# Twelve unread products of the unit matrix behind chunk 0's right sides in a recurrence-plus-MLP kernel

## The chip, the cores and the metric

The kernel runs on one core of one Trainium2 chip. The metric is the device time of one execution in microseconds (us), from the host's side of the launch to its end; for one core it is the time of that core. A profiled execution also has a span, the time from its first to its last instruction, which is a little shorter than its device time.

## What is computed

The reference runs a recurrence over 768 tokens for 4 sequences and 8 heads of width 40, and feeds its result through a two-layer block with SiLU. All arrays are float32.

```python
for t in range(S):
    y[:, :, t] = np.einsum('bhd,bhde->bhe', rt, state)
    Sa = np.einsum('bhde,bhe->bhd', state, at)
    state_decay = state * wt[:, :, None, :] - np.einsum('bhd,bhe->bhde', Sa, bt)
    state = state_decay + np.einsum('bhd,bhe->bhde', vt, kt)
x = y.transpose(0, 2, 1, 3).reshape(B * S, H * D)      # 3072 x 320
h = x @ w_in                                           # 320 -> 2048
out = (h * (1.0 / (1.0 + np.exp(-h)))) @ w_out         # 2048 -> 320
```

## The kernel before, in words

The 768 tokens are cut into 12 chunks of 64. Inside a chunk the recurrence becomes a triangular system: products of decayed inputs, an inverse of a unit triangular matrix for each of the 32 pairs of sequence and head, and an update of the state between chunks. For chunk `n` the steps are `load` and `load_r` (DMAs on SP's queue), `prepare` (scans and scalings on VectorE, small products on TensorE), `special` (the inverse for chunks 0 to 2), `inverse` and `merge` (the inverse for later chunks, two at a time), `chain` (solve and state update), `read` (the chunk's output `y`), `bring`, and `moe` (the two layers for the chunk's 256 tokens, lines 1397 to 1460). `weights` (lines 461 to 522) rebuilds float32 weights from 64-bit words that POOL's queue fetches; the first three of its ten pieces add two halves by products with the unit matrix `ident` (line 508).

Nearly all products of the recurrence are small: 40 or 64 rows by 64 columns. The products of `moe` fill the array: 128 rows, 128 columns of weights, 256 columns streamed (line 1405) or 320 (line 1445). Every product is two instructions on TensorE, a weight load and a matmul.

No step is issued where it stands in the text. `add` records each with an engine, a cost, what it reads and writes, and a priority; `plan.best(10, 400)` (line 1505) tries priorities against its own cost model, fixes one order for all engines, and gives every temporary one of four PSUM tiles `pairs[0]` to `pairs[3]` (two banks each). Lines 1504 to 1506 then issue the steps in that order, one program for each engine:

```python
    with tc.manual_schedule():
        for op in plan.best(10, 400):
            op["do"]()
```

TensorE starts in this order: for chunk 0 the decayed products with `b` and with `k` (function `between`, line 682), two batches of transposes (line 769), and the right sides (function `sv`, line 744, 64 products of the masked result with `v`); then for chunk 1 the products with `b` (line 682), and for chunk 0 transposes (926), first product (913) and refinement (958) of the inverse, the solve (1166), chunk 1's products with `k` (682), the weights' sums (508), the reading of the chunk (1269, 1323), the solve (1135), and so on. Chunk 1's first products need `a` times its decay, which VectorE makes in `prepare(1)` (`scale`, line 654, behind the scans of lines 627 and 645).

The right sides' products are recorded by the one statement that the change touches:

```python
        add("PE", 0.9, sv, [sk, ("v", i2, 0), ("v", i2, 1)], [pv, ("R", i3)], pri + 0.6, [pv, sk], 128)
```

In the order that the planner finds, `sv` of chunk 0 writes `pairs[0]`. The tile `pairs[1]` held chunk 0's products with `k` until VectorE's masking (line 729) had read them, and is next written by chunk 1's products with `b`.

Of the kernel before, what the change touches and what calls it, by code (L numbers as in the profile page):

```python
# [33 lines left out]
class Plan:  # L34
# [9 lines left out]
    def add(self, engine, cost, do, r=(), w=(), pri=0, rooms=(), k=0, size=0.0, shape="Q"):  # L44
        op = dict(
            engine=engine, cost=cost, do=do, pri=pri, rooms=rooms, k=k, size=size, n=len(self.ops), shape=shape
        )
        before = set()
        for k in r:
            if isinstance(k, tuple) and k[0] == "@":  # L50
                before.add(self.wrote[k[1]])
                continue
            if k in self.wrote:
                before.add(self.wrote[k])
            self.read.setdefault(k, []).append(op["n"])
        for k in w:
            if k in self.wrote:
                before.add(self.wrote[k])
            before.update(self.read.get(k, ()))
            self.wrote[k], self.read[k] = op["n"], []  # L60
        before.discard(op["n"])
        op["before"] = before
        self.ops.append(op)
        return op
# [224 lines left out]
def kernel(  # L289
# [15 lines left out]
    nc = tc.nc  # L305
# [26 lines left out]
    ident = const.tile([128, 128], F32, name="ident")  # L332
# [29 lines left out]
    pairs = [ps.tile([128, 2, 512], F32, name=f"pair{i}") for i in range(4)]  # L362
# [9 lines left out]
    add = plan.add  # L372
# [212 lines left out]
    def load_r(n):  # L585
        pri = 10 * n - 4
        late = [[("@", ("in", "X", 0))], [("@", ("xt", 0, 0))]][n] if n < 2 else []
        for b in range(2):
            for j in range(2):
# [17 lines left out]
                    pri,  # L607
                )

    def prepare(n):  # L610
        pri = 10 * (n - 2) + 6 if n != 1 else -8
        i3, i2 = n % 3, n % 2
# [80 lines left out]
        if n < NS:  # L693
            for b in range(2):
                for c in range(4):
                    e = "ACT" if n == 0 and b else "SP"
                    p, r = 32 * c + 16 * b, 64 * b + 16 * c
# [27 lines left out]
        pk, sk = Room("pair", 2), Room("lam", 3)  # L725
# [11 lines left out]
        pv = Room("pair", 2)  # L737
# [11 lines left out]
                    stop=True,  # L749
                )  # L750

        add("PE", 0.9, sv, [sk, ("v", i2, 0), ("v", i2, 1)], [pv, ("R", i3)], pri + 0.6, [pv, sk], 128)
        add(
            "ACT",
            act(640),
# [715 lines left out]
    load(0)  # L1471
    hold(0, at[0], [("a", 0)], 0.5)
    prepare(0)
    special(0)
    load_r(0)
    load(1)
    prepare(1)
    for n in range(5):
        weights(n)
    for n in range(NN):  # L1480
        if n >= NS:
            merge(n)
        for step in (chain, read, bring):
            ahead(step, n)
        if n == 0:
            plan.wrote["@", 0] = plan.wrote["xt", 0, 0]
            hold(4, xt[:, 0], [("xt", 0, h) for h in range(H)], 3)
            special(1)
            for i in range(5, len(units)):
                weights(i)  # L1490
        moe(n)
        if n + 1 < NN:
            load_r(n + 1)
        if n + 2 < NN:
            load(n + 2)
            prepare(n + 2)
        if n + 2 < NS:
            special(n + 2)
            if n + 3 == NS:
                eye()  # L1500
        if n + 1 >= NS and (n + 1 - NS) % 2 == 0 and n + 1 < NN:
            inverse((n + 1 - NS) // 2)

    with tc.manual_schedule():
        for op in plan.best(10, 400):
            op["do"]()

    bad = const.tile([1, 1], I32, name="bad")
    ok = sb.tile([128, 2 * NN], F32, name="ok")
# [18 lines left out]
    with tc.If(flag > 0):  # L1528
# [25 lines left out]
        with tc.For_i(0, S, T) as t0:  # L1554
# [13 lines left out]
            for t in range(T):  # L1568
                a, k, b, wt = (e4[:, x, t].unsqueeze(1).to_broadcast([128, N4, D]) for x in range(4))
# [90 lines left out]
```

## Time and profile before

| what | value |
|---|---|
| device time, median of 3 runs | 743.88 us (742.13 to 744.6) |
| profiled execution: its device time, its span | 742.53 us, 740.8 us |
| mean granted TensorE clock | 0.976 |
| busy: TensorE matmul, weight load | 674.7 us (91%), 540.5 us (73%) |
| busy: VectorE, ScalarE, GpSimd | 419.5 us (57%), 194.6 us (26%), 14.3 us (2%) |
| instructions on TensorE | 12666 weight loads and 12666 matmuls |
| chain that ended last, by engine | PE 80%, DVE 8%, DMA 3%, ACT 3%, issue 3% |
| instruction blocks fetched by DMA (queue 8) | 101 packets, 1.65 MB |

Busy time is the union of the spans of an engine's instructions; matmuls overlap each other, so a busy TensorE is not yet one at its peak. The granted clock is the share of its full clock that a throttle lets TensorE have. "Issue" is time in which an engine waited for nothing that the profile shows. The chain is followed back from the last instruction to whatever released each step.

### The profile page before, as it was taken

To read this page: it belongs to the slowest core of one execution; us is meant where nothing else is said; L and a number is where in the kernel's file an instruction comes from. 1 tells how busy PE (TensorE), PEld (TensorE's weight loads), DVE (VectorE), ACT (ScalarE), POOL (GpSimd) and SP (SyncE) were. 2 spreads that over 40 slices of the span, in tenths; PEclk is the share of its full clock that TensorE was granted. 3 is DMA by queue.
4 is the path that set the end of the run, shared out by engine and by line. 5 is a ranking of instruction groups with operands and counts; after the bars stand their busy time and mean duration, and the time that the engine had idled before them with its cause. 6 is when DMAs were issued, how large, how long until landed. Compare 5 with 4: busy or idle time off the path is not lost.

```text
span 740.8 us, 27279 instructions
## 1 busy us (share of the span) xinstructions
PE 674.7 (91%) x12666; PEld 540.5 (73%) x12666; DVE 419.5 (57%) x614; ACT 194.6 (26%) x241; POOL 14.3 (2%) x31
## 2 busy tenths in 40 slices
PE   2179799898899999999999999899999999999995
PEld 2176577678678677878778878778777778788773
DVE  6845799976479256299273397362686449321000
ACT  3251635523212411404304205124114211202020
POOL 2300000000000000000000000000000000000000
PEclk9996999999999999999999999999998999999998
DMA  7770654742632453525353506333233321401000
GB/s 248 160 227 11 195 210 126 222 116 47 161 107 58 96 135 98 139 61 125 112 133 106 161 19 144 95 99 92 73 93 81 97 60 32 126 21 41 18 1 22
DMA packets 117979, 77.15 MB, mean 104 GB/s; under 512 B 65506, under 2 KB 114338, under 8 KB 117218
## 3 DMA queue, kind: packets, MB, share of 16 engines
q1 hardware_dynamic: 113352, 64.54, 32.9%
q0 software_dynamic: 2096, 10.49, 4.3%
q8 instruction: 101, 1.65, 0.9%
q10 hardware_dynamic: 2410, 0.30, 0.3%
q14 instruction: 20, 0.16, 0.1%
HBM read 60.29 MB, written 14.61 MB: 101 GB/s over the span
## 4 chain that ended last, share of the span: by engine, by line
PE 80%; DVE 8%; DMA 3%; ACT 3%; issue 3%; SPq 1%; ACTq 1%; DVEq 0%
PE pair L1445 27%; PE pair L1405 21%; PE pair L1418 5%; PE pair L1269 4%; PE pair L682 3%; PE pair L1323 3%; PE pair L958 2%; PE pair L1135 2%; PE pair L1223 2%; PE pair L1068 1%; PE pair L1166 1%; PE pair L508 1%; PE pair L744 1%; PE pair L1308 1%; PE pair L1111 1%
## 5 line engine op out<-in xcount | busy, mean ns | idle before, releaser
L1445 PE MATMUL pair<-wo,gts 128*128 128x320 f32 x768 | 219.8, 442 | 1.1 <-issue 1.1
L1445 PEld LDWEIGHTS pair<-wo,gts 128*128 128x128 f32 x768 | 144.7, 192 | 60.4 <-issue 4.3
L1405 PE MATMUL pair<-xt,wi 128*128 128x256 f32 x768 | 175.5, 386 | 1.6 <-ACT R L756 1.3
L1405 PEld LDWEIGHTS pair<-xt,wi 128*128 128x128 f32 x768 | 145.7, 192 | 24.5 <-ACT R L756 1.4
L1428 ACT ACTIVATE gts<-pair 128x1024 f32<-128x1024 f32 x48 | 46.5, 1020 | 134.5 <-PE pair L1418 108.3
L682 PE MATMUL pair<-a,kb 40*64 40x64 f32 x1536 | 32.2, 236 | 35.8 <-DVE a L654 28.7
L1457 DVE COPY ot<-pair 128x320 f32<-128x320 f32 x24 | 11.8, 490 | 92.4 <-PE pair L1445 88.9
L796 DVE TENSOR_REDUCE XI<-XI 128x64 f32<-128x512 f32 (+9 forms) x85 | 58.6, 690 | 2.9
L682 PEld LDWEIGHTS pair<-a,kb 40*64 40x64 f32 x1536 | 28.6, 149 | 38.5 <-issue 20.5
L1418 PE MATMUL pair<-xt,wi 64*128 64x256 f32 x384 | 47.9, 389 | 0.0
L1281 DVE TENSOR_TENSOR lam<-pair,ml 128x1024 f32<-128x1024 f32 x22 | 26.4, 1220 | 32.9 <-PE pair L1269 30.4
L1418 PEld LDWEIGHTS pair<-xt,wi 64*128 64x128 f32 x384 | 35.1, 187 | 6.7 <-issue 2.6
L795 DVE TENSOR_TENSOR XI<-XI,mi 128x1024 f32<-128x1024 f32 (+8 forms) x60 | 33.6, 559 | 9.6 <-DMA mi<-md 8.3
L1334 DVE TENSOR_TENSOR lam<-pair,wz 128x1024 f32<-128x1024 f32 x11 | 13.5, 1223 | 38.8 <-PE pair L1323 38.8
L1269 PEld LDWEIGHTS pair<-r,vut 40*64 40x64 f32 x1536 | 25.9, 142 | 6.8 <-issue 5.9
L664 DVE TENSOR_TENSOR kb<-kbv 128x512 f32<-128x512 f32 (+1 forms) x36 | 29.7, 861 | 0.3
L1269 PE MATMUL pair<-r,vut 40*64 40x64 f32 x1536 | 28.5, 228 | 1.2 <-issue 1.2
L627 DVE TENSOR_TENSOR_SCAN kbv<-wz,zt 128x1024 f32<-128x1024 f32 x12 | 27.5, 2291 | 0.5
L645 DVE TENSOR_TENSOR_SCAN wz<-wz,zt 128x1024 f32<-128x1024 f32 x12 | 27.5, 2289 | 0.3
L756 ACT COPY R<-pair 128x640 f32<-128x640 f32 x12 | 8.3, 693 | 67.1 <-PE pair L744 61.5
L795 DVE TENSOR_TENSOR XI<-XI,xs 128x1024 f32<-128x1024 f32 (+1 forms) x25 | 25.3, 1010 | 0.8
L407 ACT ACTIVATE vu<-pair 64x640 f32<-64x640 f32 x13 | 9.1, 698 | 60.3 <-PE pair L1135 59.4
(151 smaller groups left out, 687.7 us busy)
## 6 DMA issues: line engine op xcount, KB each, us to landing
wz<-in_wT SPq DMA_DIRECT2D x12, 512.0 KB
kbv<-in_bT SPq DMA_DIRECT2D x12, 512.0 KB
a<-in_aT SPq DMA_DIRECT2D x12, 512.0 KB
kbv<-in_kT SPq DMA_DIRECT2D x12, 512.0 KB
r<-in_rT SPq DMA_DIRECT2D x48, 96.0 KB
vut<-in_vT SPq DMA_DIRECT2D x48, 96.0 KB
vu<-in_v SPq DMA_DIRECT2D x24, 160.0 KB
out<-ot SPq DMA_DIRECT2D x48, 80.0 KB
```

What stands on the lines that cost most here:

```text
L627: nc.vector.tensor_tensor_scan(back(V), back(W[:, 2 : 2 + Q * C]), zt, 1.0, ALU.mult, ALU.add)
L645: nc.vector.tensor_tensor_scan(Z, Z, zt, 0.0, ALU.mult, ALU.add)
L664: TTn[engine].tensor_tensor(out=at_(kb, place(is_b, first), (576 * step, 4 // step), (128, 4), (1, C)), in0=blocks((kf, bf)[is_b]), in1=bl ...
L682: nc.tensor.matmul(room.tile[half(b), j, g * C : g * C + C], lhsT=kb[rows(j), place(is_b, q) : place(is_b, q) + C], rhs=A[rows(j), q * C : ...
L795: nc.vector.tensor_tensor(out=at_(tmp, 0, *dims), in0=x, in1=y, op=ALU.mult)
L796: nc.vector.tensor_reduce(out=out_, in_=at_(tmp, 0, *dims), axis=AX.X, op=ALU.add)
L1269: nc.tensor.matmul(pl.tile[half(1 - b if role else b), b, c * C : c * C + C], lhsT=vut[rows(b), role, hu, :], rhs=rs[rows(b), hh, :], star ...
L1281: lambda pl=pl, la=la: nc.vector.tensor_tensor(out=la.tile.rearrange("p (q t) -> p q t", q=Q), in0=pl.tile.rearrange("p a b -> p (a b)").r ...
L1405: nc.tensor.matmul(rooms[g].tile[:, f // 2, (f % 2) * T : (f % 2) * T + T], lhsT=wi[:, k, (4 * g + f) * 128 : (4 * g + f) * 128 + 128], rh ...
L1418: nc.tensor.matmul(rooms[g].tile[:, h, (f % 2) * T : (f % 2) * T + T], lhsT=wi3[half(h), g * 256 + (f % 2) * 128 : g * 256 + (f % 2) * 128 ...
L1428: nc.scalar.activation(out=gts[:, 4 * g * T : 4 * g * T + 4 * T], in_=rooms[g].tile.rearrange("p a b -> p (a b)"), func=AF.Silu)
L1445: nc.tensor.matmul(po[b].tile[:, 0, 0:DM], lhsT=g4[:, f, 128 * b : 128 * b + 128], rhs=wo[:, f, :], start=f == 0, stop=f == NF - 1,)
```

## The change

A new function `idle` inside the builder issues twelve products: the 128 x 128 unit matrix as weights, and the same matrix repeated four times as the 512 streamed columns. They write the two banks of `pairs[1]` in turn, each starting afresh, and nothing reads what they write. `prepare` keeps the record of its right sides and, for chunk 0 alone, hangs `idle` on it; the loop that issues the planned order calls it directly behind that step. The planner does not know of it, so the order and the places of all other steps stay as they are, and no other instruction on any engine gains or loses a wait. TensorE's program grows by 24 instructions, 12 weight loads and 12 matmuls, behind the 224 products that stand before.

```diff
+    def idle():
+
+        for i in range(12):
+            nc.tensor.matmul(
+                pairs[1][:, i % 2].rearrange("p (a b) -> p a b", a=4),
+                lhsT=ident,
+                rhs=ident.unsqueeze(1).to_broadcast([128, 4, 128]),
+                start=True,
+                stop=True,
+            )
+
     def prepare(n):
...
-        add("PE", 0.9, sv, [sk, ("v", i2, 0), ("v", i2, 1)], [pv, ("R", i3)], pri + 0.6, [pv, sk], 128)
+        mine = add("PE", 0.9, sv, [sk, ("v", i2, 0), ("v", i2, 1)], [pv, ("R", i3)], pri + 0.6, [pv, sk], 128)
+        if n == 0:
+            mine["then"] = idle
...
     with tc.manual_schedule():
         for op in plan.best(10, 400):
             op["do"]()
+            if "then" in op:
+                op["then"]()
```

## The prediction

> **What bounds the kernel now.** I read the list of who waited for whom on TensorE first, because the change touches that engine alone, then TensorE's timeline where the new products land, then busy time in windows with the granted clock. Waits (in total, times, longest, us), over the whole span:
>
> ```profile
> PE pair L682 <- DVE a L654: 28.7, 2, 14.9
> PE pair L682 <- issue: 5.5, 6, 2.8
> PE pair L1166 <- issue: 3.2, 2, 2.8
> ...
> PE pair L1405 <- ACT R L756: 1.3, 1, 1.3
> ```
>
> TensorE has two long waits, both at the start and both for VectorE (13.79 us before its first product, 14.93 us before chunk 1's); behind them it is 91% busy and the chain runs through it. The rest that matters is "issue", 2.8 us at a time. The timeline (start, length, line; x counts products):
>
> ```profile
> 13.79 3.69 PE L682 MATMUL pair<-a,kb 40*64 40x64 f32 x128 [13.79 <-DVE a L654]
> 17.42 1.93 PE L769 MATMUL pair<-ident,kb 40*128 40x40 f32 x32
> 19.28 1.94 PE L744 MATMUL pair<-vu,lam 64*64 64x40 f32 x64
> 36.15 1.99 PE L682 MATMUL pair<-a,kb 40*64 40x64 f32 x64 [14.93 <-DVE a L654]
> ...
> 46.48 3.31 PE L958 MATMUL pair<-XI 64*64 64x64 f32 x102 [0.99 <-issue]
> ...
> 53.04 0.26 PE L1166 MATMUL pair<-X,R 64*40 64x64 f32 x3 [2.76 <-issue]
> ...
> 62.50 3.78 PE L508 MATMUL pair<-gts,ident 128*128 128x512 f32 x4
> ```
>
> The new products stand between 19.28 + 1.94 = 21.22 us and 36.15 us. The chain that ends last does not touch TensorE there: from 21.7 to 36.1 us it is VectorE alone (scans of lines 627 and 645, the inverse's steps of 795 and 796, line 654), then TensorE from 36.15 to 69.4 us.
>
> Windows of 3.41 us (length; busy us and instructions of PE, PEld, DVE, ACT, POOL; granted clock; DMA share; GB/s). I chose that width and phase because all changes of the recorded clock stand whole multiples of 3.41 us apart, at 53.27, 66.92, 77.16, 80.57 and 200.04 us:
>
> ```profile
> 32.79:36.20 3.41, 0.05 (x4) 0.05 (x4) 3.33 (x6) 0.00 (x0) 1.88 (x3) 1.00 0.63 78
> 36.20:39.61 3.41, 3.41 (x98) 3.17 (x102) 3.38 (x4) 2.29 (x4) 0.87 (x2) 1.00 0.96 301
> 39.61:43.03 3.42, 3.42 (x92) 3.23 (x90) 0.09 (x1) 3.15 (x7) 0.00 (x0) 1.00 1.03 330
> ...
> 46.44:49.85 3.41, 3.37 (x115) 3.33 (x118) 2.09 (x4) 0.05 (x1) 0.00 (x0) 1.00 1.08 265
> 49.85:53.27 3.42, 0.66 (x40) 0.50 (x34) 0.67 (x1) 0.00 (x0) 0.00 (x0) 0.99 0.34 47
> 53.27:56.68 3.41, 3.41 (x118) 3.25 (x109) 2.73 (x4) 1.19 (x2) 0.00 (x0) 0.50 0.17 43
> ...
> 63.51:66.92 3.41, 3.41 (x18) 1.37 (x18) 2.28 (x10) 0.00 (x0) 0.00 (x0) 0.51 0.00 0
> ```
>
> The column reads 1.00 before the first record, which is at 43.03 us; the products tell that it is not so. Two rows of the answer by tile say how long each lasted (minimum/median/maximum ns, first and last start in us):
>
> ```profile
> L958 PE MATMUL pair<-XI x128: 213/218/267, 44.5 to 49.6; 64*64 64x64 f32 x128
> ...
> L913 PE MATMUL pair<-mi,sb x64: 310/312/363, 39.1 to 40.8; 64*64 64x64 f32 x64
> ```
>
> Same shape, 312 against 218 ns (line 1269's, from 58.9, last 311 again): TensorE is at half clock until 43.03, full until 53.27, half until 66.92. The fall at 53.27 follows one window with 0.66 us of work; the rises took two busy windows (36.20 to 43.03) and four (53.27 to 66.92).
>
> **The products themselves.** Nearest row: line 508, also 128 rows, 128 columns of weights, 512 streamed. At half clock 3.78 / 4 = 0.945 us each (timeline above); at full clock six took 2.97 us, 0.495 each (83.53 us). Bounds for twelve: 5.9 us and 11.3 us. They wait for nothing new (`pairs[1]` was read by VectorE by 18.84 us, `ident` is used from 17.42), so they end between 27.2 and 32.6 us, at least 3.5 us before VectorE releases line 682. Cost on the path: 0. Without this cover each would cost its 0.5 to 0.95 us. They add no DMA and no wait; ScalarE's copy of the right sides hangs on the last product of line 744, ahead of them.
>
> **What they do to the clock.** The Trainium skill, "TensorE: Matmul & The Clock Gate", Part 1, says that one busy window of about 3.4 us releases the clock. The row says up to four (53.27 to 66.92), and none for the 7.4 us of small products from 13.79. By the rule the clock rises near 26 us: five and a half products at 0.945, the rest at 0.495, end near 29 us. By the slow row it never rises: end at 32.6. Either way TensorE is then idle for 3.5 to 7 us before 36.15. In this trace 2.76 us of idleness, one thin window, sufficed for the fall. So I take it that 36.15 meets half clock as before: gain 0. The ends: at worst nothing is lost; at best 36.15 to 43.03 runs at full clock. Line 682's 64 products take 1.16 instead of 1.99 us (as at 170.46 us), so 6.9 us shrink to about 4.0, 2.9 us less.
>
> What would that 2.9 be worth? The stop at 50.28 ends with an instruction fetch. From the start to it TensorE passes 128+32+64+64+16+64+16+64+26 = 474 products to the stop at 45.5, and 102+26 = 128 more, 256 instructions, to the stop at 50.28. With the few instructions that only wait, the stops stand 192 past a multiple of 256, as do those at 196 us (2.77) and some fifteen shorter ones. Each ends 1.2 to 1.6 us after a 16 KB packet of queue 8 has landed. The packet for 53.04 starts at 50.69, just when the other transfers end (DMA share 1.08 in the window before, 0.34 in this). Those transfers are weights and inputs, released at 34 us by POOL and SP. A faster TensorE would reach the stop sooner and wait for the same packet: most of the 2.9 is given back there.
>
> **The 24 instructions.** Every fetch boundary behind them comes 12 products earlier in the program. "Runtime: NRT & Kernel Launch", "Instruction fetch mechanics", calls crossing a 16 KiB boundary mostly hidden; by it the shift costs 0. The rows say 17 us of stops in the whole trace, so I recounted: all positions behind the 448th instruction raised by 24, each packet as late after its request as now, all other gaps kept. The stops sum to 13.0 us against 13.3 with the old positions counted alike. New or longer ones near 361.5 (+0.7) and 466.6 us (+0.75), shorter ones near 264, 366 and 463.6 us. An estimate of -0.3, ends -1 and +1.5 (other shifts up to 48 instructions gave that much).
>
> **Sum**: 0 + 0 - 0.3 on the profiled 742.53. That execution is 1.35 us below the median, inside the runs' own spread of 2.5; the mean of the four executions is 743.3, and I forecast 743.2 us.
>
> **Rivals.**
> *Faster, 740.3.* The clock has a memory longer than a window, and after the new products it rises sooner, or falls less deep, in the stretch to 66.92. Each window of 53.27 to 66.92 at full instead of half clock saves half of it, 1.7 us; two windows 3.4. For it: the same engine needed two windows once and four another time, so more than one window's work must count. Against it: at least 3.5 us of idleness in between. From full clock through all of 53.27 to 66.92 it would be up to 6.8.
>
> *Slower by the clock, 745.8.* The first rise took two windows, the second four. If the new products use up the first one (up near 26, down by 33 to 36 us), the rise at 43.03 may wait. Then line 958's last 174 products keep 62 ns instead of 31 (its first 18 took 1.0 us before 43.03, the next 46 took 1.4): +5.4 us up to 50.28. The stops of 0.99 and 2.76 absorb most; TensorE passes the place of 53.04 at about 54.9, +1.9, and two to three with what follows. It decides as soon as the loss exceeds the 3.75 us of stops.
>
> *Slower by the fetch, 746.5.* One lengthened stop thins a window enough to drop the clock: 196.63 to 200.04 has 1.25 us of work, and the next window runs at half clock (1.7 us lost); 244.41 to 247.82 fell with 2.53 us. Stops of 0.7 to 0.75 beside the waits near 361 and 467 us, with one or two such windows, make 0.75 + 1.7 to 3.4. It decides where work per window falls below about 2.5 us; for it the four falls behind 70 us, against it the recount's balance.
>
> *The change blocks TensorE*: a product of over 1.24 us (14.93 / 12) is needed; the longest of line 508 lasts 1.22 with its latency. I leave it at nothing.
>
> **Chances.** 0.3% of the median, 2.2 us, is about what a measurement tells from no change. No change 0.46 (0.03 faster, 0.39 same, 0.04 slower; own range 741.5 to 745.5); faster rival 0.25 (0.23, 0.02 same); slower by the clock 0.12 (0.01 same); slower by the fetch 0.17. Sums: 0.26, 0.42, 0.32. The range 740.2 to 746.8 holds the likeliest, most of the slower cases and half of the faster one.
>
> **What would show it.** Twelve matmuls of 128 x 512 from about 21.2 us, ended by 33; line 682 at 36.15 with 311 ns each (218 would be the faster rival); the first full clock near 43 (later: slower by the clock); the stop before line 1166 twelve products earlier, ended near 53; "issue" on line 682 and line 1445 of the same sum. I am wrong if the count of half-clock windows before 100 us changes by two or more, or if a stop of 2 us appears in a new place.

## The result, and the profile after

The changed kernel takes as long as the one before: ratio 1.0004, 95% interval 0.9982 to 1.0025, over 22 runs of each on the same chips; medians 740.86 and 740.59 us. Single runs of either spread from 734 to 749 us. (The ratios here and below leave out runs more than 1.5% above the fastest of their kernel.) The forecast started from three runs of the kernel before at 743.88 us; in the 22 runs beside the changed kernel it was itself 3.3 us faster, so the two have to be compared by the ratio: the forecast of 743.2 us was -0.1% of its baseline, and +0.04% was measured.

One thing in the sections above has to be put right first. A float32 product of this program is not one matmul on TensorE but two: the trace has 24 matmuls and 24 weight loads for the twelve products, and TensorE's program grew by 48 instructions, not 24. (Line 508 shows it in the trace of before: three pieces of weights with four sums each, and 24 matmuls.) The batches of 64 in the description of the kernel, and the counts x64 and x128 of the timelines, are likewise matmuls of half as many products. From here on matmuls are counted, not products.

The profile of the changed kernel is that of a run of 744.54 us, the second slowest of its 22, with a mean granted clock of 0.966, so what it shows late in the run need not be typical. The new matmuls and what follows them, on its timeline of TensorE (start, length in us; line, shape and count; idle time before):

```profile
19.20 1.94 PE L755 MATMUL pair<-vu,lam 64*64 64x40 f32 x64
21.07 11.80 PE L613 MATMUL pair<-ident 128*128 128x512 f32 x24
36.16 1.16 PE L693 MATMUL pair<-a,kb 40*64 40x64 f32 x64 [3.29 <-DVE a L665]
37.26 1.17 PE L939 MATMUL pair<-ident,mi 64*128 64x64 f32 x16
38.36 2.22 PE L926 MATMUL pair<-mi,sb 64*64 64x64 f32 x64
...
46.04 5.43 PE L971 MATMUL pair<-XI 64*64 64x64 f32 x126 [2.52 <-issue]
51.26 0.27 PE L1179 MATMUL pair<-X,R 64*40 64x64 f32 x2
53.34 0.59 PE L1179 MATMUL pair<-X,R 64*40 64x64 f32 x27 [1.81 <-issue]
```

(Lines stand 11 to 13 higher than before: 693 was 682, 926 was 913, 971 was 958, 1179 was 1166.) They fill the gap and end at 32.87 us; VectorE's release at 36.16 is the same as before, 36.15. Chunk 1's first 64 matmuls now take 1.16 us, not 1.99: the clock is full there. But the two stops for "issue" are still there, 24 matmuls earlier in the program, and they end at 46.04 and 53.34 us where they ended at 46.48 and 53.04.

The windows between the clock's changes in this run (length; busy us of PE, PEld, DVE, ACT, POOL; granted clock; DMA share; GB/s). The first record of the clock is at 23.60 us, full:

```profile
23.60:27.01 3.41, 3.41 (x9) 1.52 (x8) 3.00 (x14) 0.00 (x0) 1.99 (x3) 1.00 0.90 261
27.01:30.42 3.41, 3.41 (x9) 1.52 (x8) 3.24 (x7) 0.00 (x0) 0.00 (x0) 1.00 0.98 220
30.42:33.84 3.42, 2.46 (x6) 0.76 (x4) 3.24 (x9) 0.00 (x0) 0.00 (x0) 1.00 0.22 66
33.84:37.25 3.41, 1.08 (x64) 1.02 (x64) 3.41 (x5) 0.00 (x0) 2.10 (x3) 1.00 0.68 94
37.25:40.67 3.42, 3.42 (x91) 3.03 (x84) 2.62 (x3) 3.33 (x6) 0.97 (x2) 0.50 0.93 300
40.67:44.08 3.41, 2.85 (x82) 2.60 (x83) 1.38 (x2) 3.41 (x7) 0.00 (x0) 1.00 1.06 320
44.08:47.49 3.41, 1.45 (x49) 1.45 (x50) 0.27 (x1) 1.92 (x2) 0.00 (x0) 1.00 1.04 307
47.49:50.91 3.42, 3.42 (x72) 3.42 (x70) 1.80 (x3) 0.00 (x0) 0.00 (x0) 0.50 1.09 286
```

The clock rises 2.5 us after the first new matmul. It is kept over the pause of 3.29 us and still full at 36.16, since two windows share the pause: the one to 33.84 has 2.46 us of work, and the next, with 1.08, ends only at 37.25, where the clock falls. It is up again at 40.67, and falls once more at 47.49, behind a window that the first stop has thinned to 1.45. So the early clock was bought, and a thin window that the kernel before did not have there (its window of 43.03 to 46.44 was busy for 2.46 us) took it away again.

TensorE's longest waits between 30 and 70 us (total, times, longest), first in the changed kernel, then in the one before:

```profile
PE pair L693 <- DVE a L665: 3.3, 1, 3.3
PE pair L971 <- issue: 2.5, 1, 2.5
PE pair L1179 <- issue: 1.8, 1, 1.8
```

```profile
PE pair L682 <- DVE a L654: 14.9, 1, 14.9
PE pair L1166 <- issue: 2.8, 1, 2.8
PE pair L958 <- issue: 1.0, 1, 1.0
```

1.0 + 2.8 us of stops became 2.5 + 1.8. A third, 0.6 us, follows at 57 us.

The start of the same matmul in several kernels, in us, read off the traces. The number counts the matmuls on TensorE with those of `idle` left out; "small", "fifteen", "late" and "late + twelve" are experiments told below:

| matmul | what | before | changed | small | fifteen | late | late + twelve |
|---|---|---|---|---|---|---|---|
| 225 | chunk 1's products with b | 36.15 | 36.16 | 36.14 | 36.53 | 36.40 | 36.45 |
| 385 | first refinement, line 958 | 42.03 | 41.19 | 41.88 | 41.27 | 42.28 | 41.48 |
| 449 | second refinement | 44.46 | 43.20 | 43.89 | 44.86 | 44.64 | 43.49 |
| 605 | behind the second stop | 53.06 | 53.72 | 53.14 | 52.33 | 49.01 | 47.86 |
| 641 | | 53.92 | 54.24 | 54.10 | 52.86 | 49.53 | 48.38 |
| 855 | reading of chunk 0, line 1323 | 66.21 | 67.31 | 66.03 | 64.88 | 56.55 | 60.32 |
| 1201 | first layer of `moe` | 80.67 | 82.00 | 80.66 | 78.88 | 75.39 | 75.34 |

In these traces the changed kernel leads the one before by 1.26 us at matmul 449 and is behind by 0.66 at 605: nothing of the lead passes the stops. Even kept whole, 1.26 us is 0.17% of the time, just inside the interval, so the traces show this, and not the times.

### The profile page after: what moved, and what is told of

It reads as the page before. It is cut to its first block, busy times and chain, and to the rows that moved or that the text cites. A ratio compares the mean times of both kernels' runs of the same rounds, so it can differ in the third digit from the quotient of the medians.

```text
span 742.7 us, 27327 instructions
## 1 busy us (share of the span) xinstructions
PE 687.9 (93%) x12690; PEld 546.3 (74%) x12690; DVE 419.6 (57%) x614; ACT 194.5 (26%) x241; POOL 13.5 (2%) x31
## 4 chain that ended last, share of the span: by engine, by line
PE 78%; DVE 9%; DMA 4%; ACT 3%; issue 3%; SPq 1%; ACTq 1%; DVEq 0%
PE pair L1458 27%; PE pair L1418 20%; PE pair L1431 5%; PE pair L1282 4%; PE pair L693 3%; PE pair L1336 3%; PE pair L971 2%; PE pair L1236 2%; PE pair L1148 2%; PE pair L1081 1%; PE pair L1321 1%; PE pair L1179 1%; PE pair L508 1%; DVE kbv L638 1%; PE pair L755 1%
## 5 line engine op out<-in xcount | busy, mean ns | idle before, releaser
L1458 PE MATMUL pair<-wo,gts 128*128 128x320 f32 x768 | 222.3, 446 | 0.0
L1458 PEld LDWEIGHTS pair<-wo,gts 128*128 128x128 f32 x768 | 146.2, 194 | 60.4 <-issue 4.9
L693 PE MATMUL pair<-a,kb 40*64 40x64 f32 x1536 | 29.3, 230 | 20.1 <-DVE a L665 17.0
L693 PEld LDWEIGHTS pair<-a,kb 40*64 40x64 f32 x1536 | 26.7, 143 | 22.6 <-issue 15.8
```

Of the source, the lines that this page charges most:

```text
L693: nc.tensor.matmul(room.tile[half(b), j, g * C : g * C + C], lhsT=kb[rows(j), place(is_b, q) : place(is_b, q) + C], rhs=A[rows(j), q * C : ...
L1458: nc.tensor.matmul(po[b].tile[:, 0, 0:DM], lhsT=g4[:, f, 128 * b : 128 * b + 128], rhs=wo[:, f, :], start=f == 0, stop=f == NF - 1,)
```

## The experiments

All ratios are to the kernel before on the same chips, with 95% intervals; 22 runs each unless said.

| run | ratio | interval |
|---|---|---|
| the change | 1.0004 | 0.9982 to 1.0025 |
| e1, the twelve with 2 columns ("small") | 0.9975 | 0.9946 to 1.0003 |
| e2, 24 products | 1.0038 | 1.0012 to 1.0064 |
| e5, fifteen products | 0.9988 | 0.9962 to 1.0014 |
| e3, weights late, no products ("late") | 0.9987 | 0.9960 to 1.0014 |
| e12, the same again (14 runs) | 0.9979 | 0.9951 to 1.0006 |
| e4, weights late, twelve products | 0.9943 | 0.9917 to 0.9969 |
| e9, the same again | 0.9943 | 0.9918 to 0.9969 |
| e10, weights late, fifteen (14 runs) | 0.9998 | 0.9962 to 1.0034 |
| e11, two of three pieces late, twelve | 0.9982 | 0.9957 to 1.0006 |
| e6, pieces one by one, no products | 0.9980 | 0.9953 to 1.0007 |
| e7, pieces one by one, twelve | 0.9960 | 0.9938 to 0.9982 |
| e8, pieces one by one, fifteen | 0.9981 | 0.9957 to 1.0006 |

**e1: the instructions with little of the work.**

```diff
-                pairs[1][:, i % 2].rearrange("p (a b) -> p a b", a=4),
+                pairs[1][:, i % 2, 0:2],
                 lhsT=ident,
-                rhs=ident.unsqueeze(1).to_broadcast([128, 4, 128]),
+                rhs=ident[:, 0:2],
```

> The twelve products keep their place and their instructions, but stream 2 columns instead of 512, so TensorE has next to no work from them. Theory (the changed kernel gains by a clock that rises early and gives it back at instruction fetches): without the work the clock is at half speed again at 36.15 us, chunk 1's first products last 311 ns each, the stops before line 958 and line 1166 end near 46.5 and 53 us as in the kernel before, and the time is that of before within 0.3%. Rival (the shifted fetch boundaries by themselves cost or gain time): the time differs from before by 1 us or more, with new or longer stops at the boundaries behind 100 us.

TensorE's timeline of this run:

```profile
20.94 5.28 PE L613 MATMUL pair<-ident 128*128 128x2 f32 x24
36.14 1.99 PE L693 MATMUL pair<-a,kb 40*64 40x64 f32 x64 [9.92 <-DVE a L665]
...
45.44 4.01 PE L971 MATMUL pair<-XI 64*64 64x64 f32 x126 [1.23 <-issue]
49.31 0.30 PE L1179 MATMUL pair<-X,R 64*40 64x64 f32 x2
52.48 0.98 PE L1179 MATMUL pair<-X,R 64*40 64x64 f32 x27 [2.86 <-issue]
```

The clock is at half speed again (1.99 us for the 64), and the stops are those of before moved by 24 matmuls (1.23 and 2.86 us), ending near the same times, 45.4 and 52.5. The 24 matmuls are not quite without work: they and their weight loads still keep TensorE busy for 5.28 us, but the clock does not rise from it. Of the changed kernel's lead of 1.26 us at matmul 449 this run has 0.57 as well, because its clock happens to rise at 41.62 us and not near 43. The other 0.69 us, as far as two traces can tell, comes from the work of the new matmuls, through the clock, and not from the moved boundaries. The time is within 0.3% of before, with an interval that just takes in 1: the moved boundaries cost nothing that the times show, and whether they gain some 0.2% is not settled. In the traces all of TensorE's stops for "issue" sum to 14.1 us before, 13.0 in the changed kernel and 10.8 here.

**e2: twice as many.** `for i in range(24)`.

> 24 products instead of twelve. At full clock twelve more take some 10.4 us, so they end near 43.3 us and chunk 1's first product waits for them, 7.1 us later than now. Theory (the stretch from 36 to 53 us is set by the instruction packets, not by TensorE): most of it is absorbed, the place that the changed kernel passes at 53.3 us is passed at 55 to 56.5, and the time is 2 to 3 us above before. Rival (TensorE's work is the bound there): the place moves by 7 us and so does the time, to about 1% above before.

Chunk 1's first matmul started at 42.74 us, 6.6 later than before. At matmul 641 TensorE was still 5.1 late (59.05 us), so the stops absorbed only 1.5: the expectation of 55 to 56.5 us was wrong. Yet at matmul 855 it was 0.9 late. The clock in between was half from 50.13 to 56.95 only, two windows, where before had four up to 66.92. Neither theory had that: most of the delay was paid back by the clock, not by the packets. The time rose by 0.38%, about 2.8 us, as expected, but not for the reason that was given; where behind matmul 855 the rest of it arises was not followed.

**e5: fifteen.** `for i in range(15)`.

> Fifteen products instead of twelve: three more take 6 x 0.435 = 2.6 us at full clock, so they end near 35.5 us, half a microsecond before chunk 1's first product, and no thin window lies between. Theory (gains of this stretch are given back at the instruction packets): the clock stays full from 36.15 to 43 us (218 ns for line 682, 926 and 913 alike), TensorE comes to the stop 192 instructions past the third boundary 1 to 2 us sooner than with twelve and leaves it at the same time near 46 us, and the time is that of the changed kernel within 0.3%. Rival (one window less at half clock is worth its 1.7 us): 2 us or more below it.

```profile
36.53 1.16 PE L693 MATMUL pair<-a,kb 40*64 40x64 f32 x64 [1.32 <-DVE a L665]
37.62 0.77 PE L939 MATMUL pair<-ident,mi 64*128 64x64 f32 x16
38.32 0.69 PE L926 MATMUL pair<-mi,sb 64*64 64x64 f32 x32
39.82 0.69 PE L926 MATMUL pair<-mi,sb 64*64 64x64 f32 x32 [0.81 <-ACT sb L407]
...
44.74 0.27 PE L971 MATMUL pair<-X,XI 64*64 64x64 f32 x3 [1.51 <-issue]
...
51.83 0.27 PE L971 MATMUL pair<-XI 64*64 64x64 f32 x2 [2.79 <-issue]
```

The clock stayed full from 23 to 57 us. Two things took the gain. At full clock TensorE runs into ScalarE's copy (0.81 us before the second half of line 926), so matmul 385 starts at 41.27, no sooner than with twelve. And the stops come as before: 1.51 and 2.79 us. A third of 1.85 us follows at 54 us. The time is that of before and of the changed kernel within 0.3%, as the theory has it. Of the 1 to 2 us by which the first stop was to be reached sooner only 0.3 was seen (43.23 against 43.52 us), and it ended sooner too, at 44.74 and not near 46, so that this run keeps a lead of 0.7 to 1.8 us over the kernel before between the matmuls 605 and 1201, which the times do not show. (In this run POOL issued its 3 MB at 34.90 us, in that of the changed kernel at 36.09; whether the stop ended sooner for that was not tested.)

**e3 and e12: the packets' way cleared.** If the stops are instruction packets that wait behind data, moving the data must move the stops. POOL issues the weights' pieces 2 to 4 at 35 us and they are used from about 80 us. The same list of steps is issued, but these three behind the last step of chunk 0's inverse, with a one-column copy on POOL to wait for it:

```diff
+            if n in (2, 3, 4):
+                plan.ops[-1]["late"] = True
...
+                if n == 0 and k == 2 and part == parts[-1]:
+                    plan.ops[-1]["free"] = True
...
+            if op.get("late"):
+                held_back.append(op)
+                continue
             op["do"]()
+            if op.get("free"):
+                nc.gpsimd.tensor_copy(out=hs[:, 3:4], in_=Xs[0][:, 128:129])
+                for x in held_back:
+                    x["do"]()
```

> The kernel before, but POOL issues the weights' pieces 2 to 4 (3 MB, used from about 80 us) only when chunk 0's inverse is done near 50 us, instead of at 35 us. Theory (the packets of instructions wait behind these transfers): the third and fourth packet start within 1.5 us of their request, the stops of 0.99 and 2.76 us before lines 958 and 1166 shrink below 0.5 us each, the window before 53 us stays full, the clock does not fall there, and the time drops by 4 to 10 us. Rival (a packet takes its 3.5 us whatever else moves): both stops stay, and the time is unchanged within 0.3%. Other rival (the later weights are missed): VectorE waits for a piece at line 484 near 80 us and the time rises.

The waits of that run between 30 and 70 us, and its windows around its own clock changes:

```profile
PE pair L684 <- DVE a L656: 15.4, 1, 15.4
PE pair L1327 <- issue: 2.6, 1, 2.6
```

```profile
43.08:46.49 3.41, 3.41 (x115) 3.34 (x114) 1.98 (x3) 3.41 (x4) 0.00 (x0) 1.00 0.25 31
46.49:49.91 3.42, 3.42 (x167) 3.42 (x167) 2.54 (x5) 0.85 (x2) 0.31 (x1) 1.00 0.11 33
49.91:53.32 3.41, 3.41 (x125) 2.35 (x119) 2.80 (x8) 1.29 (x3) 2.87 (x4) 1.00 0.33 63
53.32:56.73 3.41, 3.41 (x94) 1.96 (x86) 2.85 (x5) 0.00 (x0) 0.00 (x0) 1.00 1.01 406
56.73:60.15 3.42, 0.79 (x27) 0.72 (x28) 1.40 (x6) 0.00 (x0) 0.00 (x0) 1.00 1.02 414
60.15:63.56 3.41, 3.41 (x89) 3.25 (x87) 0.00 (x0) 0.00 (x0) 0.00 (x0) 0.50 0.15 58
```

Both stops are gone, no wait of VectorE for a piece of the weights appears, and the window that before had 0.66 us of work is full. The fourth packet of instructions starts at 45.95 us instead of 50.64. TensorE leads by 4.4 us at matmul 641 and by 9.7 at 855, the last before its own stop. But where the 3 MB now run (DMA share 1.01 and 1.02, over 400 GB/s), the packet due there is late in its turn: a stop of 2.63 us at 56.8 us (one matmul later the lead is 6.8), a window of 0.79 us of work, and a fall of the clock. At matmul 1201 the lead is 5.3 us (7.0 in e12), at 2001 still 4.9 (6.4), and at 2501, near 160 us, 1.1 (2.4). In between both runs have two windows at half clock that the kernel before does not have; of e3:

```profile
128.41:131.82 3.41, 3.41 (x9) 2.24 (x8) 3.39 (x4) 2.86 (x3) 0.00 (x0) 0.50 0.65 191
135.24:138.65 3.41, 1.03 (x28) 0.86 (x28) 3.21 (x3) 1.19 (x2) 0.00 (x0) 1.00 0.98 305
138.65:142.06 3.41, 3.41 (x8) 2.11 (x7) 3.10 (x11) 0.00 (x0) 0.00 (x0) 0.50 0.96 309
```

The second row is again a window thinned to 1.03 us beside 305 GB/s; in it stands a stop of 2.58 us (2.86 in e12) at line 1312, where the kernel before has 0.91. So of the expected 4 to 10 us of time 0.1 to 0.2% is left, with intervals that take in 1. That the packets wait behind the transfers is shown: the stops went where the 3 MB went. That the kernel gets faster by the delay alone is not.

The second measurement was made as the counterpart of e9, though on another chip:

> The kernel before with the weights' pieces 2 to 4 together behind chunk 0's inverse, a second time. If the twelve products are worth 2 to 3 us once the packets are in time, the ratio to before is again 0.997 to 1.0, against 0.9943 of both runs with products; if the delay alone does it, it is near 0.994.

**e4 and e9: late weights and the twelve products.** The edit of e3 on the changed kernel.

> The changed kernel with the same delay of the weights' pieces 2 to 4. Theory: with the packets no longer late the early clock is kept, TensorE reaches the place of 53.3 us 1 to 3 us before the kernel with late pieces and no products, and the time is 1 to 3 us lower than that one's. Rival (the twelve products are worth nothing even then, because VectorE or ScalarE ends the waits of that stretch): the two are equal within 0.3%.

> The twelve products with the weights' pieces 2 to 4 together behind chunk 0's inverse, a second time and on the chip that this call gets. If the gain is real, the ratio to before is again 0.991 to 0.997; if the first time was luck with the clock's windows, it lies at 0.998 or above.

In e4 the clock falls once at 37.55, as in the changed kernel, and is then full from 40.97 to 58.03 us, over the place where it was lost: matmul 605 starts at 47.86 us, 5.9 before the changed kernel. It starts 0.6 to 1.6 us sooner in e4 and e9 than in e3 and e12. One wait of 3.2 us at line 1286, the late packet, stands in the place of the earlier stops:

```profile
PE pair L1286 <- issue: 3.2, 1, 3.2
PE pair L695 <- DVE a L667: 3.2, 1, 3.2
```

In e9 the clock does not fall near 37 us at all. The pause before line 695 lies so that the two windows that share it keep 1.91 and 2.20 us of work, where e4's have 2.48 and 1.11. From matmul 225 to 385 e9 takes 4.74 us and e4 5.03, so the window at half clock costs about 0.3 us here and not 1.7: as in e5, TensorE then waits for ScalarE's copy (0.80 us).

Both times the kernel is 0.57% faster than before, some 4 us, and both intervals lie below 1 and below that of the changed kernel. How much of it the twelve products add is less firm: 0.9943 twice against 0.9987 and 0.9979 without them, with intervals that overlap; on the one chip that ran both e3 and e4 the medians are 739.9 and 738.1 us.

Nor is it shown that the early clock is what they add. Behind the late packet the early lead is gone: at matmul 870 e4 and e9 are 1.2 to 3.5 us behind e3 and e12, because the boundary moved by 48 instructions puts the stop ahead of the last matmuls of the reading and not behind them; at 1201 they are level to 2.1 us behind. They come out ahead later: from matmul 2001 to 3000, about 120 to 177 us, e4 and e9 take 53.9 and 53.5 us, e3 and e12 both 57.1. TensorE's stops for "issue" there are 0.2 and 2.1 us against 4.3 and 4.4 (e4 has a wait of 2.3 us for a DMA besides). That points to the moved boundaries rather than to the clock of the first 50 us. Late weights with the small products of e1 would tell the two apart; this was not run, and the question stays open.

**e6, e7, e8, e10, e11: smaller transfers, other counts.** In e6 to e8 the three pieces are released one at a time, behind chunk 0's inverse, its first masked reading and its first scaled half (three values of `free`, the rest as in e3); e10 has fifteen products with the pieces as in e4; e11 leaves piece 2 at 35 us.

> The kernel before, with the weights' pieces 2, 3 and 4 issued one by one: when chunk 0's inverse is done (47 us), when its first masked reading is done (53), and when its first half is scaled (61). Theory (3 MB at once hold a packet back by 3 us wherever they are put; 1 MB by at most 1): the stop of 2.6 us that stood at 56.8 us with the three together falls below 1 us, and the time is 1 to 3 us below that of the three together. Rival (any transfer ahead of a packet costs the same, or a late piece is missed at line 484): no lower.

> The changed kernel with the pieces issued one by one as in the run without products. Theory: TensorE passes product 854 (the last sum of line 508 before line 1323) near 55 us, the clock falls at most once between 38 and 70 us, and the time is 1 to 3 us below the same kernel without products and below the one with three pieces together. Rival (behind 70 us the chain waits for other things and takes the lead back): equal to the three together within 0.3%, although product 854 comes earlier.

> Pieces one by one, and fifteen products. Theory: with the packets in time, the window at half clock near 38 us is gone and is worth up to 1.7 us here, unlike with the pieces at 35 us: 0.5 to 2 us below twelve products with the pieces one by one. Rival (VectorE and ScalarE set the pace of chunk 0's inverse at full clock): equal to twelve.

> The same with fifteen products. Theory: the window at half clock near 38 us goes, TensorE passes product 640 about 1 us sooner than with twelve, but the stop behind product 829 (53.5 to 56.8 us with twelve) ends with its packet behind the 3 MB; since these start when chunk 0's inverse is done, the stop moves with it and up to 1 us is kept: 0 to 1 us below twelve. Rival: a whole window, 1.7 us or more.

> Twelve products; piece 2 stays at 35 us, pieces 3 and 4 (2 MB) go behind chunk 0's inverse. Theory (a packet waits for about 3 us per MB ahead of it): the stop near 44 us is below 1 us, the stop near 53.5 us shrinks from 3.2 to about 2, and the time is within 0.3% of that with all three late. Rival (what counts is whether any bulk transfer lies before 46 us): the stops of 2 us and more near 43.5 and 51.5 us come back and the time is that of the changed kernel.

Spreading did not help: e7 is faster than the kernel before too (0.9960), but its median is 736.9 us, and that of e6, without products on the same chip, 737.3. Without products the stop near 56.4 us fell to 0.71, as expected, but stops of 1.95 and 3.58 us came at 60.8 and 65.9. With products a stop of 2.97 us stood at 53.4, and then the first layer of `moe` waited 4.2 us near 70 us for its input `xt`: the third piece, issued at 64.7 us, ran just then, and one transfer of `xt` took 6.75 us. With piece 2 left early, stops of 1.1, 1.5 and 1.4 us appeared. Fifteen products beat twelve neither with the pieces together nor one by one; e10 is no better than before, where 0 to 1 us below twelve was expected. All five intervals overlap that of e4, so no more is read from their order than that e4 was not improved on. Of the expectations e6's on the stop near 56 us held, and e7's on the clock, which fell once between 38 and 70 us. e7's matmul 854 came at 59.2 us and not near 55, and the gains of e6, e7 and e8 over the versions beside them did not show. e11 missed its own: its time is 0.39% above that of e9 on the same chip, where 0.3% at most was expected, though the intervals overlap.

## Why the prediction was right

The time and "no change" came out as forecast, by a path that differed in two of its steps. One of the stated signs of being wrong came true: the windows at half clock before 100 us, by the records, went from 5 to 7. (A stop of over 2 us came as well, 2.52 us, but at the place of the old first stop, 24 matmuls earlier.) So the time was right and the account of the clock was not.

- *The products cost nothing on the path*: right, line 693 starts at 36.16. Its size was wrong. I took line 508's 0.945 and 0.495 us for a product, and they are for a matmul, half a product. By those rows the bounds should have been 11.9 and 22.7 us; measured 11.80, just below both, since the new matmuls start 0.43 us apart at full clock and 0.85 at half. At 0.85 throughout, an estimate from this trace, they would have ended near 41.7 us, 5.6 too late. So the cover held only because the clock rose at 23.60, and the rival "blocks TensorE", which I left at nothing, was decided by that: a product takes two matmuls, 1.7 us at half clock, over its limit of 1.24. The prediction had not counted on that rise; here it was lucky. e2 shows its price: 6.6 us at the start of chunk 1, 2.8 at the end.
- *The clock is at half speed again at 36.15*: wrong. It follows from the size: with 24 matmuls the pause is 3.3 us, not 3.5 to 7, and no window of 3.41 us fell wholly into it. The 64 matmuls took 1.16 us, which I had put down as the mark of the faster rival. That the time stayed has to do with how little the clock was worth: 0.69 us at matmul 449 beyond e1, not 2.9.
- *The gain would be given back at the stops*: right for the changed kernel. The 2.9 us at best were 1.26 at matmul 449, and less than nothing at 605; e3 shows what the stops wait for. e5 has the same stops with a clock that never fell in between, and there 0.7 to 1.8 us were kept in the trace.
- *The moved boundaries*: 48 instructions, not 24. The recount said -0.3 us, with ends -1 and +1.5; e1 says -0.25% (-0.54 to +0.03), so no loss. My count can't be told right or wrong closer than that. "Issue" on the old lines 682 and 1445 was to keep its sum; it went from 5.5 and 1.1 us to 1.5 and none, as the stops moved to other lines. Three figures were off, without weight for the result: the rows of the wait list add up to 14.1 us of stops, not 17; 743.3 less 0.3 is 743.0, not 743.2; and the 91% busy is of the whole span, behind the two long waits it is 95%.
- *The rivals*: the first full clock came 20 us earlier and the later rise was not delayed for it (40.67 instead of about 43), which rules out "slower by the clock" as it was put. A related thing did happen: the second fall at 47.49, behind a stop of 2.52 us. It began 0.7 us sooner than in e1, with the faster clock, and ended 0.6 later. Of "slower by the fetch" nothing shows in the time.

## What to carry to other kernels

Warming up an engine is worth only what the next thing it waits for leaves over; look for that wait, and count how long it lasts if the engine comes sooner. Where stops that the profile calls "issue" stand at equal distances in the count of instructions, look for packets of instructions that land just before they end, as here: see which bulk transfer runs just then and whether that transfer is needed so early. And take the duration of an operation from a row only after checking how many of the trace's instructions one operation of the source makes.

## What was not expected of the hardware

- The clock rose 2.5 us after the first full-size matmul (1.6 to 3.6 in the other runs that have these), while 7.4 us of small ones (13.8 to 21.2 us) did not raise it in the kernel before. In e1 even 12.6 us without a pause, small ones and then 24 of two columns, did not. So a busy TensorE alone, as the profile counts it, did not raise the clock. The later rise took four windows of mixed work (54.32 to 67.97 us).
- Packets of 16 KB (0.9 to 1.6 us long) were held up for microseconds by some 3 MB of other transfers, at both places where these were put: the third and fourth started 2.2 and 4.7 us sooner in e3 than before (41.76 and 45.95 us against 43.91 and 50.64, of which 1 us is the first stop's own), and the sixth, beside the moved transfers, only at 57.11.
- Runs of one kernel differ by up to 2.5%, and most of it goes with the granted clock: over 75 runs of the kernel before, on one chip, time and mean clock have a correlation of -0.79, about 6 us for 0.01. A window at half clock is 0.0023 of that mean, so runs differ by several such windows, and an effect of 1 us in the first 60 us is below what a single profile can decide.
